# The pieces of the last weight matrix in another order, and three of them converted from shifted bytes

## The chip, the cores and the metric

The kernel runs on one core of one Trainium2 chip. The metric is the device time of one execution in microseconds. The median of three runs of the kernel before is 475.51 us (475.21 to 475.67).

## The reference: what is computed

Three stages follow each other: attention with soft-capped scores, a feed-forward layer with a softmax-like activation and a layer norm, and a gated feed-forward layer. The change lies in the last one:

```python
def _moe2_ref(x, w_gate, w_val, w_out):          # x 896 x 768, w_gate and w_val 768 x 1536, w_out 1536 x 768
    g = x @ w_gate
    silu = g * (1.0 / (1.0 + np.exp(-g)))
    val = x @ w_val
    return (silu * val @ w_out).astype(np.float32)
```

The weights come as float64 numbers, and the output is float32.

## The kernel before, in words

TensorE multiplies every pair of float32 operands as a high and a low part, each rounded to the engine's format: high by high, high by low, low by high, three matmuls for one (`mm3`). So each operand is split: `hi` is a rounding copy on ScalarE, `lo` a subtraction on VectorE.

A weight tile is 128 x 768 float64 numbers, about 768 KB. It takes four steps to become float32. `load_shifted` (L166) issues the DMA on SyncE's queue, leaving out the first three bytes, so that the wanted bits stand in aligned words. Then two ScalarE activations with the function Prelu make sign and exponent out of the top byte, and one VectorE `SCALAR_TENSOR_TENSOR` ORs the mantissa in (`f32_shifted`, L180). The other way, `load64` with `f32_steps` (L103, L114), is a plain load, one ScalarE absolute value, and on VectorE two `TENSOR_SCALAR` (clamp and shift) and two `SCALAR_TENSOR_TENSOR` (sign and mantissa). `b22`, the last quarter of w_out2, went this way, in three pieces (0, 2 and 4).

In the last third of the kernel the bytes land in a pool with two buffers named `raw`, and the float32 values in one with two buffers named `f32` (`self.st`, L1191). Pieces take the two in turn. The DMA of a piece therefore waits for the `SCALAR_TENSOR_TENSOR` of the piece two places ahead of it, and its first Prelu for the splits of that piece.

The hidden dimension of 1536 is worked on in 12 blocks (`fc`). For the last three (9, 10, 11) the loop at the end of `run` multiplies x by the block's gate weights (`g`) and value weights (`v`): 18 matmuls of 384 columns for each, then 18 of 512 for each. The weights of block 11 (`wg`, `wv` below) are loaded by `load_gv` (L624) while block 10 is multiplied, through the same two `raw` buffers as the pieces of w_out2 that `load_w2` (L939) fetches. The table `early` (L1264) says which piece is loaded in which half of which block, and so sets the one order of all these loads:

```python
early = {9: ((6, 8), (0,)), 10: ((1,), (2,)), 11: ((3, 4), (5, 10))}
...
    elif fc + 1 < K2:
        self.load_gv(fc + 1, i)
    for c in early[fc][i]:
        self.load_w2(c)
    self.ff2_gv(fc, N, o)
```

A scheduler orders the instructions of ScalarE and VectorE by times that it assumes; each engine then works them off strictly in that order, and TensorE's order is the program's.

The output product (`ff2_out`, L980) is a seven-product scheme on 2 x 2 blocks (products p1 to p7, for three row tiles and a seventh half). p1 uses the pieces 0 to 5 (`b11`), p2 the pieces 6, 8 and 10 (`b21`). Beside the products, VectorE makes sums and differences of operands; p6 needs the last of them (`so`, `t`). The three pieces of `b22` are converted during the first products (`conv`).

Of the kernel before, what the change touches and what calls it, by code (L numbers as in the profile page):

```python
# [56 lines left out]
class Kernel:  # L57
# [898 lines left out]
    def load_b22(self, k):  # L956

        src = self.w_out2[(self.KD + k) * 128:(self.KD + k + 2) * 128, self.HN:].rearrange("(f p) d -> p f d", p=128)
        self.b22raw[k] = self.load64(src, f"b22_{k}")

    def f32_b22(self, k):

        f = self.B22f[:, k:k + 2].rearrange("p f d -> p (f d)")
        self.f32(self.b22raw.pop(k), f"b22_{k}", f=f)

    def split_b22(self, k):

# [179 lines left out]
    def run(self):  # L1147
# [18 lines left out]
        w = [self.w_in_steps(i) for i in range(KD)]  # L1166
        f, g, hi, lo = zip(*w)
# [49 lines left out]
        wb, gb = self.wb, _ = self.pool("wb"), self.pool("gb")  # L1217
# [10 lines left out]
        for j in range(2, KD):  # L1228
# [4 lines left out]
            a, b = x2[j]  # L1233
# [27 lines left out]
        self.sg = (self.ee[:, :n], self.ee[:, n:n + 512])  # L1261
        self.T1f = [self.ee[:, n + 512 + n * i:n + 512 + n * (i + 1)] for i in range(3)] + [t1, self.sms]
        self.t1 = t1
        early = {9: ((6, 8), (0,)), 10: ((1,), (2,)), 11: ((3, 4), (5, 10))}  # L1264
        for fc in range(K2):
            if fc == 0:
                self.ff2_gv_first()
# [66 lines left out]
```

## Time and profile before

| | |
|---|---|
| median of 3 runs | 475.51 us |
| profiled execution: device time | 475.99 us |
| profiled execution: span of instructions | 474.2 us |
| TensorE busy | 466.7 us, 98% of the span |
| VectorE busy | 387.8 us, 82% |
| ScalarE busy | 310.4 us, 65% |

The span runs from the first to the last instruction; 1.8 us of the device time lie outside it. Times in the rows below are microseconds from the start of the span. In a row, a tile's name stands without its number: `w<-w_raw` is a piece of w_out2, `wg` and `wv` the gate and value weights, `b` the b22 quarter.

### The profile page before, as it was taken

Reading aid. Unit: us, or ns where it says so; the run is one execution under the profiler, and the core shown is the slowest. Engines: PE = TensorE matmul, PEld = TensorE weight load, DVE = VectorE, ACT = ScalarE, POOL = GpSimd, SP = SyncE. Lnnn points to the kernel's source line nnn. Section 1 sums busy time; section 2 is a strip of 40 time slices with the busy share of each in tenths; the row PEclk is TensorE's granted clock in tenths of the full one; section 3 lists DMA queues with packets and bytes.
Section 4 is the critical chain, followed back from the end, with each engine's and each line's share of the span. In section 5 each row is a group of like instructions: output and inputs, shape, how many; then the busy total and the mean of one; then the engine's idle time right before and its main releaser. Section 6 shows DMA issues by size and latency. Waiting matters only on the chain.

```text
span 474.2 us, 7675 instructions
## 1 busy us (share of the span) xinstructions
PE 466.7 (98%) x2970; PEld 384.8 (81%) x2970; DVE 387.8 (82%) x669; ACT 310.4 (65%) x455; POOL 38.7 (8%) x76
## 2 busy tenths in 40 slices
PE   9999999999999999999999999999999999998997
PEld 7444454447888899989989999999999889998996
DVE  3689999987778996866778899989876768999993
ACT  4999999951223799887767766766667778344220
POOL 1011010112000000000012222220000000000000
PEclk9999999999999999999999999999999999999999
DMA  6786575002000225345225444331445757010003
GB/s 181 170 207 153 163 193 153 21 2 88 1 1 0 90 88 165 126 129 180 66 81 185 134 134 132 109 122 37 132 128 155 241 182 221 7 50 18 17 19 132
DMA packets 65060, 52.33 MB, mean 110 GB/s; under 512 B 35584, under 2 KB 61952, under 8 KB 64256
## 3 DMA queue, kind: packets, MB, share of 16 engines
q1 hardware_dynamic: 64992, 51.85, 36.7%
q8 instruction: 23, 0.38, 0.3%
q14 instruction: 13, 0.11, 0.1%
q0 software_dynamic: 32, 0.00, 0.0%
HBM read 49.09 MB, written 2.75 MB: 109 GB/s over the span
## 4 chain that ended last, share of the span: by engine, by line
PE 80%; DVE 10%; DMA 5%; ACT 4%; issue 1%; ACTq 0%; DVEq 0%; SPq 0%
PE x L49 12%; PE h L49 12%; PE p L49 8%; PE g L49 8%; PE pv L49 8%; PE sc L49 7%; PE b L49 6%; PE c L49 6%; PE S L49 4%; DMA w_raw<-in_moe_w_out_dram 3%; PE e L49 3%; DVE b L49 2%; ACT w L49 2%; PE v L49 2%; DVE so L49 1%; PE lt L49 1%
## 5 line engine op out<-in xcount | busy, mean ns | idle before, releaser
L49 PE MATMUL g<-x,g 128*128 128x448 f32 (+2 forms) x288 | 62.2, 365 | 0.0
L49 PE MATMUL h<-wi,x 128*128 128x512 f32 x252 | 59.2, 393 | 0.0
L49 PEld LDWEIGHTS g<-x,g 128*128 128x128 f32 x288 | 53.1, 188 | 5.4 <-ACT ee L49 0.3
L49 PEld LDWEIGHTS h<-wi,x 128*128 128x128 f32 x252 | 46.8, 188 | 11.3 <-issue 1.5
L49 ACT ACTIVATE P<-sc,consts 112x896 f32<-112x896 f32 x48 | 45.4, 1010 | 3.8 <-PE sc L49 2.2
L49 ACT ACTIVATE P<-P,consts 112x3584 f32<-112x3584 f32 (+1 forms) x13 | 39.7, 3060 | 0.1
L49 PE MATMUL pv<-P,v 112*32 112x448 f32 x384 | 38.5, 540 | 0.0
L49 PEld LDWEIGHTS sc<-ks 64*112 64x112 f32 x288 | 23.3, 171 | 18.3 <-issue 8.4
L49 PE MATMUL sc<-ks 64*112 64x448 f32 x288 | 35.8, 379 | 0.3
L49 PE MATMUL x<-lB,wo 128*128 128x256 f32 (+1 forms) x192 | 35.2, 337 | 0.0
L49 PEld LDWEIGHTS x<-lB,wo 128*128 128x128 f32 x192 | 29.6, 189 | 3.4
L49 PE MATMUL b<-a,g 128*128 128x448 f32 x144 | 31.9, 366 | 0.0
L49 ACT ACTIVATE ee<-h,sms 128x512 f32<-128x512 f32 x14 | 9.5, 685 | 33.2 <-DVE sms L49 33.2
L49 PEld LDWEIGHTS pv<-P,v 112*32 112x32 f32 x384 | 12.2, 110 | 23.0 <-issue 20.9
L49 PE MATMUL v<-x,g 128*128 128x384 f32 (+1 forms) x144 | 30.4, 362 | 0.3 <-DVE g L49 0.3
L49 PEld LDWEIGHTS b<-a,g 128*128 128x128 f32 x144 | 27.0, 188 | 2.3 <-DVE ee L49 0.2
L49 PEld LDWEIGHTS v<-x,g 128*128 128x128 f32 x144 | 26.0, 188 | 3.5 <-DVE g L49 0.7
L49 PE MATMUL x<-lA,wo 128*128 128x384 f32 x144 | 27.2, 338 | 0.0
L49 PEld LDWEIGHTS x<-lA,wo 128*128 128x128 f32 x144 | 25.2, 188 | 0.5
L49 POOL COPY sm<-tr 32x14 f32<-32x14 f32 x48 | 15.0, 312 | 93.1 <-DVE tr L49 91.6
L49 PE MATMUL S<-P,ones 112*32 112x448 f32 x192 | 22.4, 549 | 0.0
L49 DVE TENSOR_TENSOR x<-x,x 128x448 fp32r<-128x448 f32 (+3 forms) x26 | 15.3, 588 | 8.3 <-ACT x L49 7.6
(273 smaller groups left out, 967.6 us busy)
## 6 DMA issues: line engine op xcount, KB each, us to landing
wg_raw<-in_moe_w_gate_dram SPq DMA_DIRECT2D x12, 765.8 KB, 4.3
wv_raw<-in_moe_w_val_dram SPq DMA_DIRECT2D x11, 765.8 KB, 4.7
wi_raw<-in_moe_w_in_dram SPq DMA_DIRECT2D x6, 1024.0 KB, 7.7
w_raw<-in_moe_w_out_dram SPq DMA_DIRECT2D x6, 767.6 KB, 4.2
wo_raw<-in_moe_w_out_dram SPq DMA_DIRECT2D x6, 512.0 KB, 3.5
wo_raw<-in_moe_w_out_dram SPq DMA_DIRECT2D x6, 510.5 KB, 3.6
v<-in_v_dram SPq DMA_DIRECT2D x24, 112.0 KB, 4.0
kq<-in_k_dram SPq DMA_DIRECT2D x22, 112.0 KB, 3.0
```

The costliest lines, as they stand in the source:

```text
L49: i = f(*a, **k)
```

## The change: what it does

The table `early` gets another order: 0, 1, 2, 3, then 6, 8, 4, 5, 10. The pieces of `b22` are loaded by `load_shifted` and converted by two Prelu and one `SCALAR_TENSOR_TENSOR` in place of the five instructions.

```diff
     def load_b22(self, k):
 
         src = self.w_out2[(self.KD + k) * 128:(self.KD + k + 2) * 128, self.HN:].rearrange("(f p) d -> p f d", p=128)
-        self.b22raw[k] = self.load64(src, f"b22_{k}")
+        self.b22raw[k] = self.load_shifted(src, f"b22_{k}")
 
     def f32_b22(self, k):
 
         f = self.B22f[:, k:k + 2].rearrange("p f d -> p (f d)")
-        self.f32(self.b22raw.pop(k), f"b22_{k}", f=f)
+        raw, o = self.b22raw.pop(k), {}
+        self.shifted_steps(o, "b", lambda: raw, lambda: f)
+        for w in "12f":
+            o["wb" + w]()
...
-        early = {9: ((6, 8), (0,)), 10: ((1,), (2,)), 11: ((3, 4), (5, 10))}
+        early = {9: ((0, 1), (2, 3)), 10: ((6,), (8,)), 11: ((4, 5), (10,))}
```

SyncE's queue, from the first piece of w_out2 on; `w_6_raw` is piece 6, `wg_raw` and `wv_raw` are the weights of block 11, minus is before and plus is now:

```order
-L177 DMA w_6_raw<-in_moe_w_out_dram 128x2x3069
-L177 DMA w_8_raw<-in_moe_w_out_dram 128x2x3069
 L173 DMA w_0_raw<-in_moe_w_out_dram 128x6141
-L177 DMA wg_raw<-in_moe_w_gate_dram 128x6x1021
 L173 DMA w_1_raw<-in_moe_w_out_dram 128x6141
-L177 DMA wv_raw<-in_moe_w_val_dram 128x6x1021
 L173 DMA w_2_raw<-in_moe_w_out_dram 128x6141
 L173 DMA w_3_raw<-in_moe_w_out_dram 128x6141
+L177 DMA wg_raw<-in_moe_w_gate_dram 128x6x1021
+L177 DMA w_6_raw<-in_moe_w_out_dram 128x2x3069
+L177 DMA wv_raw<-in_moe_w_val_dram 128x6x1021
+L177 DMA w_8_raw<-in_moe_w_out_dram 128x2x3069
```

`wg` moves from the fourth place to the fifth, and `wv` from the sixth to the seventh; after these rows come 4, 5, 10 and the three pieces of b22 in both kernels.

ScalarE before, from the first Prelu of `wg` to the rounding copy of `wv` (`g_2` and `g_3` are the tiles that TensorE reads for block 11, `ee<-g` is a Silu, `a<-` and `kR<-` are rounding copies):

```order
L49 ACTIVATE wg_3605<-wg_raw,consts 128x768
L49 ACTIVATE a_2486<-w_0_3553 128x384
L49 ACTIVATE wg_3605<-wg_3605,consts 128x768
L49 ACTIVATE g_2_1930<-wg_3605 128x768
L49 ACTIVATE a_2486<-ee 128x384
L49 ACTIVATE w_1_3613<-w_1_raw,consts 128x768
L49 ACTIVATE w_1_3613<-w_1_3613,consts 128x768
L49 ACTIVATE ee<-g_384_3679 128x512
L49 ACTIVATE wv_3664<-wv_raw,consts 128x768
L49 ACTIVATE a_2486<-w_1_3613 128x384
L49 ACTIVATE wv_3664<-wv_3664,consts 128x768
L49 ACTIVATE g_3_1931<-wv_3664 128x768
```

The same stretch now, from the first Prelu of piece 6, which stands between the second Prelu of `wg` and the copy of `wg`:

```order
L49 ACTIVATE w_6_3620<-w_6_raw,consts 128x768
L49 ACTIVATE g_2_1930<-wg_3612 128x768
L49 ACTIVATE w_6_3620<-w_6_3620,consts 128x768
L49 ACTIVATE wv_3672<-wv_raw,consts 128x768
L49 ACTIVATE kR<-w_6_3620 128x384 x2
L49 ACTIVATE a_2486<-ee 128x512
L49 ACTIVATE wv_3672<-wv_3672,consts 128x768
L49 ACTIVATE ee<-g_0_3749 128x384
L49 ACTIVATE w_8_3680<-w_8_raw,consts 128x768
L49 ACTIVATE g_3_1931<-wv_3672 128x768
```

Before, nothing that waits for a transfer stood between the second Prelu of `wg` or `wv` and its copy. Now the first Prelu of piece 6 stands ahead of the copy of `wg`, and that of piece 8 ahead of the copy of `wv`; three rounding copies stand between the two Prelu of `wv`, where there was one.

## Rows read from the trace of the kernel before

**Rows 1.** The page: busy time by engine, and granted clock of 40 slices

```profile
PE 466.7 (98%) x2970; PEld 384.8 (81%) x2970; DVE 387.8 (82%) x669; ACT 310.4 (65%) x455; POOL 38.7 (8%) x76
...
PEclk9999999999999999999999999999999999999999
```

**Rows 2.** Waits of TensorE, 330 to 476: total us, times, longest

```profile
PE p L49 <- DVE so L49: 2.0, 1, 2.0
PE p L49 <- DVE g L49: 0.7, 1, 0.7
PE v L49 <- DVE g L49: 0.3, 1, 0.3
```

**Rows 3.** Timeline of TensorE: start, us, engine, line, operation, [idle before]

```profile
373.90 3.31 PE L49 MATMUL g<-x,g 128*128 128x384 f32 x18
377.05 0.52 PE L49 MATMUL v<-x,g 128*128 128x384 f32 x2
377.91 3.05 PE L49 MATMUL v<-x,g 128*128 128x384 f32 x16 [0.34 <-DVE g L49]
...
392.68 0.62 PE L49 MATMUL p<-g,a 128*128 128x384 f32 x2 [0.66 <-DVE g L49]
...
433.35 0.98 PE L49 MATMUL p<-t,so 128*128 128x384 f32 x4 [2.04 <-DVE so L49]
```

**Rows 4.** Timeline of SyncE's DMA queue, the first six loads

```profile
349.16 1.77 SPq L177 DMA_DIRECT2D w_raw<-in_moe_w_out_dram  x2
356.73 0.35 SPq L173 DMA_DIRECT2D w_raw<-in_moe_w_out_dram  x1
360.91 0.37 SPq L177 DMA_DIRECT2D wg_raw<-in_moe_w_gate_dram  x1
365.34 0.35 SPq L173 DMA_DIRECT2D w_raw<-in_moe_w_out_dram  x1
368.43 0.37 SPq L177 DMA_DIRECT2D wv_raw<-in_moe_w_val_dram  x1
```

**Rows 5.** Timeline of ScalarE around the first Prelu of `wg`, and the copy of `wv`

```profile
362.88 0.61 ACT L49 ACTIVATE a<-ee 128x512 fp32r<-128x512 f32 x1
363.40 0.92 ACT L49 ACTIVATE w<-w,consts 128x768 int32<-128x768 f32 x1
...
365.18 1.00 ACT L49 ACTIVATE wg<-wg_raw,consts 128x768 f32<-128x768 int8 x1 [0.48 <-DMA wg_raw<-in_moe_w_gate_dram]
366.07 0.52 ACT L49 ACTIVATE a<-w 128x384 fp32r<-128x384 f32 x1
366.49 0.93 ACT L49 ACTIVATE wg<-wg,consts 128x768 int32<-128x768 f32 x1
...
376.01 0.85 ACT L49 ACTIVATE g<-wv 128x768 fp32r<-128x768 f32 x1 [1.02 <-DVE wv L49]
```

**Rows 6.** Timeline of VectorE: the mantissa step of the first two pieces, of `wg` and `wv`

```profile
355.75 0.96 DVE L49 SCALAR_TENSOR_TENSOR w<-w_raw,w 128x768 uint32<-128x768 uint32 x1 [2.42 <-ACT w L49]
...
359.92 0.96 DVE L49 SCALAR_TENSOR_TENSOR w<-w_raw,w 128x768 uint32<-128x768 uint32 x1 [0.21 <-ACT w L49]
...
367.45 0.96 DVE L49 SCALAR_TENSOR_TENSOR wg<-wg_raw,wg 128x768 uint32<-128x768 uint32 x1 [0.27 <-ACT wg L49]
...
375.02 0.96 DVE L49 SCALAR_TENSOR_TENSOR wv<-wv_raw,wv 128x768 uint32<-128x768 uint32 x1 [0.27 <-ACT wv L49]
...
376.89 0.96 DVE L49 TENSOR_TENSOR g<-wv,g 128x768 fp32r<-128x768 f32 x1 [0.31 <-ACT g L49]
```

**Rows 7.** Timeline of VectorE: a piece of b22, and the step that p6 waits for

```profile
396.32 1.15 DVE L49 TENSOR_SCALAR b<-b 128x768 f32<-128x768 f32 x2 [0.42 <-ACT b L49]
397.51 1.95 DVE L49 SCALAR_TENSOR_TENSOR b<-b_raw,b 128x768 uint32<-128x768 uint32 x2
...
432.35 3.56 DVE L49 TENSOR_TENSOR so<-s,so 128x768 fp32r<-128x768 f32 x4
```

**Rows 8.** Busy time of each engine and granted clock, two stretches

```profile
351.00:395.00 44.00, 43.00 (x212) 37.95 (x211) 29.51 (x46) 32.02 (x46) 0.00 (x0) 1.00 0.64 214
396.00:433.00 37.00, 35.31 (x203) 34.73 (x201) 36.37 (x55) 21.10 (x36) 0.00 (x0) 1.00 0.21 65
```

## The prediction

> **What bounds the kernel now.** I read the page first. TensorE is busy for 466.7 of 474.2 us, so a change here can win only its few waits [rows 1]. Next the list of TensorE's waits over the last 146 us: there are three, 3.04 us together [rows 2]. Then the timeline, to see where they stand [rows 3]. At 377.91 the third matmul of block 11's value product waits 0.34 us for the low part of `wv`. At 392.68 p1 waits 0.66 us for the low part of piece 5. At 433.35 p6 waits 2.04 us for VectorE. The first two are the end of the stream of loads. The third is the end of a long VectorE chain, since that engine is busy for 36.37 of the 37 us from 396 to 433 [rows 8], and TensorE goes on when the first of four `so<-s` steps that begin at 432.35 has ended [rows 7].
>
> What limits the stream? Its loads go out one by one, from 349 to 368 six of them [rows 4], and each waits for the mantissa step of the piece two places ahead: that of the first piece begins at 355.75 and the third load goes out at 356.73; that of `wg` begins at 367.45 and `wv` goes out at 368.43 [rows 4, 6]. So both buffers are always in use, and a piece's place in the order decides when it is ready.
>
> **The conversion of b22.** Each of three pieces loses two `TENSOR_SCALAR` (1.15 us together) and one of two `SCALAR_TENSOR_TENSOR` (1.95 - 0.96) [rows 6, 7]: 2.14 us, 6.4 us in all from a chain that is late by 2.04. ScalarE's one absolute value becomes two Prelu, which adds about one second Prelu of 0.93 us for each piece [rows 5], 2.8 in all, to an engine that is busy for 21.10 of these 37 us [rows 8]. Even if all 2.8 stood in VectorE's way, 3.6 would be left, more than 2.04. I take the 2.04 as won, and zero as the other end.
>
> **The order: `wg`.** I follow the two buffers with intervals from start to start. Load to first Prelu 4.3 (360.91 to 365.18); first Prelu to the next instruction 0.9; a copy of 384 columns 0.42 and of 512 columns 0.52; second Prelu to mantissa step 0.96; mantissa step to the next load, or to the copy, 0.98; copy of 768 columns to its subtraction 0.88; subtraction to TensorE 1.02 [rows 3 to 6].
>
> - First buffer: piece 0 in place of piece 6, mantissa step at 355.75 as before. Piece 2 goes out at 356.73, its Prelu begin at 361.0 and (behind a copy of 512) 362.4, its mantissa step at 363.4. `wg` goes out at 364.4 (before: 360.91), its Prelu begin at 368.7 and (behind a copy of 384) 370.0, its mantissa step at 371.0.
> - Second buffer: piece 1 in place of piece 8 has one copy less ahead of its second Prelu, so 359.92 becomes 359.5. Piece 3 goes out at 360.5, with mantissa step at 367.1; piece 6 goes out at 368.1, with its first Prelu at 372.4.
> - That Prelu stands ahead of the copy of `wg`: 373.3, subtraction 374.2, TensorE 375.2. It comes to that matmul at 374.25 (373.90 and two matmuls). It loses 0.9 us.
>
> **The order: `wv`.** It goes out at 371.0 + 0.98 = 371.95 (before: 368.43), and its first Prelu begins at 376.25. Behind three copies (0.42, 0.42, 0.52) the second begins at 378.5; the mantissa step follows at 379.5. Its copy is queued behind the first Prelu of piece 8, which went out after piece 6's mantissa step (375.05) at 376.0 and lands at 380.3. So the copy begins at 381.2, the subtraction at 382.1, and TensorE's third matmul at 383.1. Without waits that matmul would have begun at 377.57 [rows 3]. It is late by 5.5 us, where it was late by 0.34: 5.2 us more, the loss at `wg` included, since the same matmuls stand behind both. The same steps on the old order give 377.98, where the row has 377.91, so I trust the method to half a microsecond. TensorE would then stand empty for about 4.2 us in one piece.
>
> Bounds: if no copy and no foreign Prelu stood in ScalarE's way, each round of a buffer would be 4.3 + 0.9 + 0.96 + 0.98 = 7.1 us, and the matmul would begin at 380.1, 2.2 us more than before. With 0.3 us more on each of the three loads that lead to `wv` in its buffer it would be 384.0, 6.1 more.
>
> **What the delay swallows.** Places 9 to 11 still hold pieces 4, 5 and 10, and by the same steps piece 5's mantissa step begins at 390.6, about where it was. TensorE comes to it 5 us later, so the 0.66 us go. At p6 it comes 4.5 us later, and VectorE, by the paragraph on b22, earlier: the 2.04 go if either holds. VectorE's start into the chain slips by about 1.2 us, since ScalarE's first Prelu of b22 is queued behind the copy of the late block's result; 6.4 covers it. Behind p6 TensorE ran 37 us without a wait, with VectorE further behind than it will be now, so I expect none there.
>
> The sum, against the profiled execution: 474.2 + 5.2 - 0.66 - 2.04 = 476.7 us of span, and with 1.8 outside it 478.5. That execution was 0.48 above the median, so in medians 475.51 + 2.5 = 478.0 us.
>
> **Rivals.**
>
> 1. The clock falls while TensorE stands empty. Every slice and stretch here shows the full granted clock, 2.4 GHz [rows 1, 8], but TensorE never waited longer than 2.04 us in this stretch, and 4.2 us is twice that. The 16 matmuls left of that product take 2.77 us (16 x 0.173); at the lower level, 1.2 GHz, they would take twice that, and nothing behind them is left to swallow it: 478.0 + 2.8 = 480.8. If it lasted into the next product (4.1 us), up to 484.9.
>    The Trainium skill, "TensorE: Matmul & The Clock Gate", Part 1: The HAM clock gate, says that the array passes to its lower rate after TensorE has been idle, and comes back after sustained work. By that rule the stall could cost more than its own length; no row of this trace shows such a fall.
> 2. The stall is short and the change wins. It decides at 380.6: if TensorE gets the low part of `wv` earlier than that, the new delay is under 2.7 us, less than the two waits that go. With the unhindered bound (380.1, +2.2) the time is 475.51 + 2.2 - 2.7 = 475.0. For it speaks that the landing of a load may be shorter when rows are contiguous (pieces 0 to 3); against it that both engines work in the order shown, with foreign work in the way.
> 3. The 2.04 us are not won: the VectorE chain, which feeds on TensorE's results and on ScalarE's three added Prelu, slips with them. Then 478.0 + 2.0 = 480.0. Against it stand 6.4 us less work and a later TensorE.
>
> **How the numbers follow.** The forecast has a chance of 0.60, with its own range of 476.8 to 479.2 (the method's half microsecond and the spread of landings); the clock 0.22; the short stall 0.10; the third 0.08. The likeliest gives 478.0. The range for 8 in 10 is 475.8 to 481.2: it takes in the first and third rival as priced, and leaves out most of the second and a longer fall of the clock. A measurement of this kernel can tell 0.2%, 0.95 us, from no change. Of the second rival's tenth, 0.06 is faster by more than that and 0.04 is same; with 0.01 of the forecast's lower edge: faster 0.07, same 0.05, slower 0.88.
>
> **What would show it.** In the profile after, TensorE's list of waits has `v` for `g` on top, over 4 us, and no `so` at p6. `wv` goes out near 372 and its mantissa step begins near 379.5. VectorE's `TENSOR_SCALAR` on `b` are gone. The granted clock in the 8 us behind the stall tells the first rival. I am wrong if `wv` reaches TensorE before 380.6, or if a wait at p6 stays.

## The result and the profile after

The changed kernel takes 479.21 us (median of 22 runs), the kernel before 476.79 us in 22 runs taken beside it: a ratio of 1.0053, 95% interval 1.0036 to 1.0069. On the median of the first runs that is 475.51 x 0.0053 = +2.5 us, with an interval of +1.7 to +3.3; the prediction had +2.5. The profiled execution has a span of 476.8 us in place of 474.2. The size is right; part of the way there is not.

The page after, busy time and granted clock by slice, which answers to [rows 1]:

```profile
PE 467.7 (98%) x2970; PEld 385.9 (81%) x2970; DVE 381.8 (80%) x660; ACT 313.0 (66%) x458; POOL 38.6 (8%) x76
...
PEclk9999999999999999999999999999999989999999
```

VectorE has lost 6.0 us, ScalarE has gained 2.6. One slice of the clock, the 33rd (381.4 to 393.4 us), is no longer full. TensorE's waits after 330 us, as in [rows 2]:

```profile
PE v L49 <- ACT g L49: 3.9, 1, 3.9
PE g L49 <- DVE g L49: 0.4, 1, 0.4
```

The wait at p6 is gone, and so is that for piece 5. In their place `v` waits 3.9 us for the high part of `wv`, and `g` 0.4 for the low part of `wg`. TensorE's timeline after, as in [rows 3]:

```profile
344.12 3.31 PE L49 MATMUL g<-x,g 128*128 128x384 f32 x18
...
373.34 0.62 PE L49 MATMUL g<-x,g 128*128 128x384 f32 x2
374.34 3.05 PE L49 MATMUL g<-x,g 128*128 128x384 f32 x16 [0.38 <-DVE g L49]
381.30 5.81 PE L49 MATMUL v<-x,g 128*128 128x384 f32 x18 [3.91 <-ACT g L49]
386.94 4.28 PE L49 MATMUL g<-x,g 128*128 128x512 f32 x18
...
395.14 1.23 PE L49 MATMUL p<-a,a 128*128 128x384 f32 x6
...
420.13 9.52 PE L49 MATMUL p<-so 128*128 128x384 f32 x54
...
435.73 1.20 PE L49 MATMUL p<-t,so 128*128 128x384 f32 x6
436.77 1.20 PE L49 MATMUL p<-so 128*128 128x384 f32 x6
```

The places in the kernel before that these are compared with:

```profile
344.97 3.31 PE L49 MATMUL g<-x,g 128*128 128x384 f32 x18
...
380.79 4.28 PE L49 MATMUL g<-x,g 128*128 128x512 f32 x18
...
388.99 1.23 PE L49 MATMUL p<-a,a 128*128 128x384 f32 x6
...
391.10 0.92 PE L49 MATMUL p<-g,a 128*128 128x384 f32 x4
...
393.14 1.20 PE L49 MATMUL p<-a,a 128*128 128x384 f32 x6
...
415.20 9.52 PE L49 MATMUL p<-so 128*128 128x384 f32 x54
...
430.80 0.51 PE L49 MATMUL p<-t,so 128*128 128x384 f32 x2
...
434.17 1.21 PE L49 MATMUL p<-so 128*128 128x384 f32 x6
```

Block 9, ahead of all that the change moves, begins at 344.12 in place of 344.97: this execution is 0.85 us early by then. I take that as chance, since in the nine profiles of this document the same row begins anywhere from 343.74 to 345.70. From there:

- Block 11's first two products take from 373.05 (373.90 less 0.85) to 386.94, 13.89 us; before, 373.90 to 380.79, 6.89. Lost: 7.0.
- p1 and p2 take 24.99 us (395.14 to 420.13); before 26.21. Won: 1.22.
- The first six matmuls of p6 take 1.04 us; before 3.37. Won: 2.33.
- 7.0 - 1.22 - 2.33 - 0.85 = 2.6, the difference of the spans.

Why are 18 matmuls of `v` slow, 5.64 us to the next product where they take 3.1 otherwise? Busy time and granted clock of four stretches after (us; PE, PEld, DVE, ACT, POOL busy, granted clock, DMA share, GB/s):

```profile
375.00:379.00 4.00, 2.39 (x14) 2.07 (x12) 3.32 (x7) 3.55 (x6) 0.00 (x0) 1.00 0.66 196
379.00:381.30 2.30, 0.01 (x1) 0.01 (x1) 0.60 (x2) 1.77 (x3) 0.00 (x0) 0.57 0.34 60
381.30:386.00 4.70, 4.70 (x14) 4.21 (x15) 2.83 (x4) 3.57 (x5) 0.00 (x0) 0.50 0.71 251
386.00:390.00 4.00, 4.00 (x20) 3.45 (x19) 2.95 (x5) 2.65 (x4) 0.00 (x0) 0.98 0.65 176
```

The clock fell to 0.50, its lower level of 1.2 GHz, while TensorE stood empty, and was full again near 386. The prediction's first rival came true. This agrees with the rule that the prediction cites (the Trainium skill, "TensorE: Matmul & The Clock Gate", Part 1: The HAM clock gate): idle time takes the clock down, and sustained work brings it back.

The load of `wv` after, in SyncE's queue, as in [rows 4],

```profile
371.15 0.37 SPq L177 DMA_DIRECT2D wv_raw<-in_moe_w_val_dram  x1
```

ScalarE from the first Prelu of `wv` to its copy, as in [rows 5],

```profile
375.41 1.01 ACT L49 ACTIVATE wv<-wv_raw,consts 128x768 f32<-128x768 int8 x1 [1.29 <-DMA wv_raw<-in_moe_w_val_dram]
...
377.67 0.92 ACT L49 ACTIVATE wv<-wv,consts 128x768 int32<-128x768 f32 x1
...
379.53 0.98 ACT L49 ACTIVATE w<-w_raw,consts 128x768 f32<-128x768 int8 x1 [0.57 <-DMA w_raw<-in_moe_w_out_dram]
380.41 0.83 ACT L49 ACTIVATE g<-wv 128x768 fp32r<-128x768 f32 x1
```

and VectorE, as in [rows 6, 7]:

```profile
378.62 0.96 DVE L49 SCALAR_TENSOR_TENSOR wv<-wv_raw,wv 128x768 uint32<-128x768 uint32 x1
381.28 0.96 DVE L49 TENSOR_TENSOR g<-wv,g 128x768 fp32r<-128x768 f32 x1 [1.70 <-ACT g L49]
...
430.02 3.57 DVE L49 TENSOR_TENSOR so<-s,so 128x768 fp32r<-128x768 f32 x4
```

With the 0.85 us added, `wv` goes out at 372.0 (forecast 371.95), its mantissa step begins at 379.47 (379.5), its subtraction at 382.13 (382.1). The copy at 380.41 begins when the first Prelu of piece 8, which waited for its transfer, is over; by the interval of 0.98 us from mantissa step to copy it could have begun at 379.60, so ScalarE's order cost some 0.8 us of the delay. No run tests that part by itself. At p6 VectorE's step begins at 430.02, and TensorE comes there at 435.73.

### The profile page after: what moved, and what is told of

Read it like the earlier page. It is cut to its first block, busy times and chain, and to the rows that moved or that the text cites. A ratio compares the mean times of both kernels' runs of the same rounds, so it can differ in the third digit from the quotient of the medians.

```text
span 476.8 us, 7667 instructions
## 1 busy us (share of the span) xinstructions
PE 467.7 (98%) x2970; PEld 385.9 (81%) x2970; DVE 381.8 (80%) x660; ACT 313.0 (66%) x458; POOL 38.6 (8%) x76
## 4 chain that ended last, share of the span: by engine, by line
PE 90%; DMA 5%; ACT 2%; DVE 2%; issue 0%; SPq 0%; ACTq 0%
PE p L49 16%; PE x L49 12%; PE h L49 12%; PE g L49 9%; PE pv L49 7%; PE sc L49 6%; PE b L49 6%; PE c L49 6%; PE S L49 4%; DMA w_raw<-in_moe_w_out_dram 4%; PE v L49 4%; PE e L49 3%; ACT w L49 2%; DMA kq<-in_q_dram 1%; PE lt L49 1%; PE T L49 1%
## 5 line engine op out<-in xcount | busy, mean ns | idle before, releaser
L49 PE MATMUL v<-x,g 128*128 128x384 f32 (+1 forms) x144 | 32.6, 382 | 3.9 <-ACT g L49 3.9
L49 PEld LDWEIGHTS v<-x,g 128*128 128x128 f32 x144 | 27.9, 202 | 7.5 <-ACT g L49 4.2
```

The lines of the kernel that those rows point to most:

```text
L49: i = f(*a, **k)
```

## The experiments

The theory A: the order puts `wv` one place back in a stream that both buffers limit; TensorE stands empty, the clock falls, and the new conversion of b22 takes away only the wait at p6. The rival B: the added Prelu on ScalarE cost the time late in the kernel.

**The order alone.**

```diff
-        early = {9: ((6, 8), (0,)), 10: ((1,), (2,)), 11: ((3, 4), (5, 10))}
+        early = {9: ((0, 1), (2, 3)), 10: ((6,), (8,)), 11: ((4, 5), (10,))}
```

> The new order of the pieces alone, b22 converted as before. Theory A (the loss is TensorE's stall on wv and the clock that falls in it; the new conversion of b22 only removes the wait at p6): the stall of about 4 us on wv and the lower granted clock behind it are there as in the changed kernel. TensorE comes to p6 some 5 us later than before, and VectorE's chain, which starts about 1 us later, still ends first, so the wait at p6 is gone without the new conversion: +2 to +3 us against the kernel before (ratio 1.004 to 1.006), the same as the full change. Theory B (the two Prelu of b22 on ScalarE cost time late in the kernel): about 1 us or more faster than the full change.

Measured: 1.0050 (1.0030 to 1.0069). TensorE's waits, and the clock in a stretch behind the longest:

```profile
PE v L49 <- ACT g L49: 3.9, 1, 3.9
...
PE v L49 <- DVE g L49: 0.4, 1, 0.4
PE g L49 <- DVE g L49: 0.3, 1, 0.3
```

```profile
382.00:384.00 2.00, 1.62 (x6) 1.30 (x6) 1.53 (x2) 0.93 (x3) 0.00 (x0) 0.56 0.79 310
```

The same stall, a fall of the clock again, and no wait at p6 although b22 is converted as before. The fall is shorter in this execution than in the profile of the changed kernel (mean clock 0.996 against 0.993); the medians are alike (479.13 and 479.21). B is out: the order makes up the whole loss, and beside it the new conversion wins nothing that these runs can tell, since a late TensorE no longer waits for VectorE.

**The conversion alone**: the changed kernel with the old line of `early`.

> The new conversion of b22 alone, the pieces in the old order. Theory A: wv and piece 5 as before (waits 0.34 and 0.66 us stay), the wait of 2.04 us at p6 is gone: -2.0 to -2.4 us against the kernel before (ratio 0.995 to 0.996). Theory B: no gain or a loss, 1.000 or more.

Measured: 473.36 us, 0.9933 (0.9910 to 0.9956), faster than both kernels. TensorE's waits after 330 us:

```profile
PE p L49 <- DVE g L49: 0.7, 1, 0.7
PE v L49 <- DVE g L49: 0.4, 1, 0.4
PE p L49 <- ACT g L49: 0.3, 1, 0.3
```

VectorE's step at p6:

```profile
428.72 3.56 DVE L49 TENSOR_TENSOR so<-s,so 128x768 fp32r<-128x768 f32 x4
```

p6's wait is gone; the waits for `wv` and piece 5 stay, with 0.3 us more for the high part of piece 5. The gain is 3.2 us by the ratio (2.1 to 4.3), where 2.0 to 2.4 was expected. From the first matmul of block 9 (343.76 here) to the end, the two profiled executions differ by 2.0 us, as expected. The rest may be the clock: all of this kernel's 6 runs have a mean granted clock of 0.999 or 1.000, where the kernel before often has less (the last experiment).

VectorE has some 6 us less to do, but counted from block 9 its step at p6 begins only 2.4 us earlier (84.96 us behind block 9's start, before 87.38). That is just enough for the wait of 2.04. Part of the rest goes into waits of 0.90 and 0.91 us for ScalarE's Prelu of the second and third piece.

**A third order with the new conversion.**

```diff
+        early = {9: ((0, 1), (2,)), 10: ((), (3,)), 11: ((4, 5), (6, 8, 10))}
```

> The new conversion of b22, and a third order: 0, 1, 2, wg, wv, 3, 4, 5, 6, 8, 10, so that wg stands at place 4 and wv at place 5 (before: 4 and 6; changed: 5 and 7), piece 5 at place 8 (10). Theory A (the place in the order decides when a piece is ready): wv is ready about 4 us ahead of TensorE, piece 5 about 8 us ahead, p6 does not wait: no wait of TensorE in the last 146 us, granted clock full, -3.5 to -4.2 us against the kernel before (ratio 0.991 to 0.993). Theory B: like the new conversion with the old order or slower, since the place of wv is of no weight.

Measured: 474.35 us, 0.9959 (0.9931 to 0.9988), less gain than expected and none over the conversion alone. The only wait after 330 us, and VectorE's step that ends it:

```profile
PE p L49 <- DVE so L49: 1.5, 1, 1.5
```

```profile
429.68 3.55 DVE L49 TENSOR_TENSOR so<-s,so 128x768 fp32r<-128x768 f32 x4
```

`wv` and piece 5 wait no more, as A says, but TensorE, now earlier, waits at p6 again. My forecast took VectorE's chain as out of the way, and it was so only for a TensorE that came late. Counted from block 9 (344.72 here), VectorE's step is 2.42 us earlier than in the kernel before, as with the conversion alone, and TensorE comes to p6 1.85 us earlier: 2.04 - 2.42 + 1.85 = 1.47, the wait that the row shows. Of the 11 runs compared, 6 have a full mean clock (0.998 or more) and a median of 473.3, the other 5 a lower one and 476.7.

**The changed kernel with the stall filled** with matmuls whose product nobody reads:

```diff
-        ps = [self.gv_product(fc, i, N, o) for i in range(2)]
+        ps = [self.gv_product(fc, 0, N, o)]
+        if fc == 11 and o == 0:
+            z = self.pt.tile([128, 512], F32, name="fill", tag="m")
+            for _ in range(16):
+                self.PE.matmul(z, self.gvs[fc][0][:, 0, 0, :], self.x2[0][:, 0, 384:896], start=True, stop=True)
+        ps.append(self.gv_product(fc, 1, N, o))
```

> The changed kernel with 16 matmuls of 512 columns, whose product nobody reads, between block 11's gate product and its value product (some 3.5 us of TensorE's time, where it stood empty for 3.9). Theory A1 (the granted clock fell because TensorE stood empty): it stays full, wv's first matmul begins when it did, and the 18 matmuls of that product take 3.1 us in place of 5.6: 1.5 to 2.5 us less than the changed kernel, +0 to +1 against before (ratio 1.000 to 1.002). Theory A2 (the product is slow for another reason, such as the weights arriving late): no change against the changed kernel, 1.005.

Measured: 477.35 us, 1.0012 (0.9996 to 1.0028) against before, by the two ratios some 1.9 us less than the changed kernel. TensorE's timeline and the clock:

```profile
378.08 3.83 PE L49 MATMUL fill<-x,g 128*128 128x512 f32 x16
382.40 0.62 PE L49 MATMUL v<-x,g 128*128 128x384 f32 x2 [0.49 <-ACT g L49]
383.40 3.04 PE L49 MATMUL v<-x,g 128*128 128x384 f32 x16 [0.38 <-DVE g L49]
386.28 4.28 PE L49 MATMUL g<-x,g 128*128 128x512 f32 x18
```

```profile
378.00:382.40 4.40, 3.91 (x18) 2.90 (x16) 2.33 (x5) 3.60 (x7) 0.00 (x0) 1.00 0.62 211
382.40:386.20 3.80, 3.42 (x18) 3.10 (x19) 2.84 (x4) 2.70 (x5) 0.00 (x0) 1.00 0.61 200
```

`wv` is as late as before the filling, but the product takes 3.9 us to the next one in place of 5.64. So the slow matmuls came from the idle time, not from late weights. Counted from block 9 (344.91 here), block 11's first two products end 5.55 us later than in the kernel before, where the changed kernel has 7.0.

**The third order with the old conversion.** The edit is the third `early` line in the kernel before.

> The third order (0, 1, 2, wg, wv, 3, 4, 5, 6, 8, 10) with the old conversion of b22. Theory A, with what the last runs add (once wv and piece 5 are early, VectorE's chain to p6 is what ends last): the waits at wv and piece 5 are gone and come back at p6, which waits for 3.5 to 4.5 us; VectorE's last step ahead of p6 ends when it did before. No gain: ratio 0.999 to 1.001 if the granted clock stays full, up to 1.005 where it falls in that wait. Theory C (the early weights are a gain of their own): 0.996, as with the new conversion.

Measured: 1.0018 (0.9999 to 1.0037): no gain, as A says. But the wait is not where I put it. TensorE's waits, VectorE's splits of piece 10, and the clock in that wait and behind it:

```profile
PE p L49 <- DVE g L49: 2.8, 1, 2.8
PE p L49 <- ACT g L49: 1.3, 1, 1.3
```

```profile
405.86 1.02 DVE L49 TENSOR_TENSOR g<-w,g 128x384 fp32r<-128x384 f32 x2
```

```profile
402.60:406.40 3.80, 0.45 (x1) 0.19 (x1) 3.80 (x8) 3.23 (x7) 0.00 (x0) 1.00 0.46 182
406.40:411.00 4.60, 4.54 (x17) 4.54 (x18) 4.46 (x8) 1.58 (x3) 0.00 (x0) 0.63 0.01 4
```

p2 waits for piece 10, whose splits stand behind those of the sums in both engines' order. VectorE, busy for all of the 3.80 us, still ends last, at another of its steps, and the clock falls again (0.63).

**The sums' splits ahead of b22's first conversion**, with the third order and the new conversion.

```diff
-            ("p1_0", 0, ((A11, b11),), (do(conv, 0),), copy(P1[0])),
-            ("p1_1", 1, ((A11, b11),), (do(s1, 0), do(s1, 2)), copy(P1[1])),
-            ("p1_2", 2, ((A11, b11),), (do(s1, 4),), copy(P1[2])),
+            ("p1_0", 0, ((A11, b11),), (do(s1, 0), do(s1, 2)), copy(P1[0])),
+            ("p1_1", 1, ((A11, b11),), (do(s1, 4),), copy(P1[1])),
+            ("p1_2", 2, ((A11, b11),), (do(conv, 0),), copy(P1[2])),
```

> The third order and the new conversion, and in the output product the splits of the sums (so), which need no piece of b22, stand ahead of the conversion of b22's first piece in place of behind it. Theory A: VectorE does these 6 us of splits while it would wait for pieces 10 and b22, its chain to p6 ends 2 to 4 us earlier, p6 does not wait, and no wait is left in the last 146 us: 1.5 to 2.5 us less than the third order alone, ratio 0.990 to 0.993 against the kernel before, and all runs at full granted clock. Theory D (ScalarE or the loads hold the chain, not VectorE's order): same as the third order alone, 0.996.

Measured: 478.24 us, 1.0031 (1.0011 to 1.0051), slower than the third order alone, which neither theory had. VectorE's timeline, TensorE at p6, and the clock behind that wait:

```profile
402.56 0.96 DVE L49 SCALAR_TENSOR_TENSOR w<-w_raw,w 128x768 uint32<-128x768 uint32 x1 [0.24 <-ACT w L49]
...
408.85 0.96 DVE L49 SCALAR_TENSOR_TENSOR b<-b_raw,b 128x768 uint32<-128x768 uint32 x1 [3.71 <-ACT b L49]
```

```profile
434.82 1.65 PE L49 MATMUL p<-t,so 128*128 128x384 f32 x4 [3.64 <-DVE so L49]
```

```profile
434.80:438.00 3.20, 3.17 (x10) 3.18 (x11) 3.20 (x4) 1.23 (x3) 0.00 (x0) 0.52 0.00 0
```

The splits fill VectorE's idle time, but they also push piece 10's conversion back to 402.56 (395.54 in the third order alone). Its buffer is what b22's second piece loads into, so that piece comes late, VectorE idles 3.71 us, p6 waits 3.64, and the clock falls. It is the buffer rule once more, through another piece.

**The kernel before, with p6's wait filled.**

```diff
+            if nm == "p6_0":
+                z = self.pt.tile([128, 512], F32, name="fill", tag="m")[:, :n]
+                for _ in range(11):
+                    self.PE.matmul(z, B22[0][0][:, :128], B22[0][0], start=True, stop=True)
             self.products(acc, A, B() if callable(B) else B, t, start, evict is not None)
```

> The kernel before, with 11 matmuls of 384 columns, whose product nobody reads, in front of p6, where TensorE waited 2.04 us for VectorE. Theory E (in about half of the runs of the kernel before the mean granted clock is 0.995 or 0.996 and the time is about 1 us longer, since the clock falls in this wait): the mean clock is 0.999 or more in all runs, and the median falls by 0.5 to 1 us: ratio 0.998 to 0.999. Theory F (the clock falls elsewhere in these runs): the clocks as before, ratio 1.000 to 1.001.

Measured: 475.65 us, 0.9979 (0.9955 to 1.0002). In 10 of 12 runs the mean clock is 0.999 or more; of 57 runs of the kernel before that were taken with the experiments, 26 have 0.998 or more (median 476.1 us) and 31 less (477.3). TensorE's timeline:

```profile
431.50 2.07 PE L49 MATMUL fill<-a 128*128 128x384 f32 x11
433.40 1.59 PE L49 MATMUL p<-t,so 128*128 128x384 f32 x6
```

This fits theory E: the wait at p6 takes the clock down in about half of the runs. The interval just reaches 1, two runs still have 0.996, and the one profile of the kernel before shows a full clock behind this wait (1.00 from 433.4 to 436), so it is likely, not shown.

## Why the prediction was right, point by point

- **The stream and its two buffers**: right. `wv`'s steps came within 0.1 us of the forecast, counted from block 9, and ScalarE's order held its copy back as forecast (381.26, forecast 381.2).
- **The new delay at `wg` and `wv`**: forecast 5.2, measured 7.0; the stall in it 4.2, measured 3.9. The mis-sized term is the speed behind the stall, where I left the clock full in the likeliest case and gave its fall 0.22. The fall came. With the stall filled the delay is 5.55, near the forecast; the fall is worth some 1.5 us between these two profiles and 1.9 in the runs.
- **The waits that go**: forecast 0.66 + 2.04 = 2.70, measured 1.22 + 2.33 = 3.55. The idle time that the timeline puts ahead of a row is less than the matmuls lose: in the kernel before six matmuls of p1 took 2.04 us (391.10 to 393.14) in place of 1.04, and six of p2, at 404.58, lost another 0.22.
- **b22**: worth 0.67% alone, but this term was too large. VectorE has 6.0 us less to do, but the prediction counted 6.4 as time won at p6, and 3.6 if all of ScalarE's added work stood in the way. Measured, the step at p6 begins 2.42 us earlier with the conversion alone, and 1.48 in the changed kernel (85.90 us behind block 9's start), since the new order alone makes it 2.0 later, where 1.2 was forecast. The 1.48 are less than the 2.04, so by these numbers the conversion would not have taken away the whole wait if TensorE had not come late; no run shows that. The late TensorE takes it away without the conversion, as the order alone shows, so in this change the conversion won nothing. The prediction, which said that either would do, did not say whose the gain would then be.
- **The sum**: 7.0 - 3.55 is 3.45 us in the two profiled executions, after taking out 0.85 us of chance at the start, and 2.5 in the runs. Two errors of opposite sign, 1.8 and 0.85, cancel by half. The other half, 0.95, is not in the medians: if half of the runs of before lose 1.2 us to the clock at p6, as the last experiment suggests, their median (476.79) stands above the profiled execution (475.99), and the difference is smaller. That is likely, not shown. The direction was earned; that the number fits to a tenth of a microsecond is luck.
- **The rivals**: the first came true in its mechanism, at some 1.9 us where it was priced at 2.8; the second (a short stall) and the third (p6 keeps its wait) did not.

## What to carry to other kernels

When two buffers in turn feed a stream of loads, a piece's place is its due time; count places (here about 3.9 us each: in the changed kernel eleven mantissa steps begin between 354.87 and 393.85) for what the bound engine needs next before giving a place ahead of it to pieces needed later. A wait removed in front of the bound engine is worth only what the next chain allows: the early weights won nothing with the old conversion (1.0018) and nothing over the new one (0.9959 against 0.9933), since TensorE then waits for VectorE; and the shorter chain won nothing while the weights were late. Work taken off an engine is not time won at the end of its chain: 6 us less work made the VectorE step that p6 needs only 2.4 us earlier. TensorE's stall of 3.9 us cost some 1.9 us more than its length, because the clock was down when it ended; price a stall of that size so.

## What the runs showed of the hardware that I had not expected

A stall of 3.9 us took the granted clock to 0.50, and it stayed there for some 5 us of dense matmuls; in all 22 runs of the changed kernel the mean clock was 0.991 to 0.996. A wait of 3.64 us at p6 took it to 0.52, and two waits of 1.3 and 2.8 us with one matmul between them to 0.63 in the stretch behind. Behind the single waits of 2.04 us (the kernel before) and 1.5 us (the third order) the profiles show it full. Yet 31 of 57 runs of the former and 5 of 11 of the latter have a lower mean clock, at a cost of 1.2 and 3.4 us between the medians. That these waits bring it down in part of the runs is likely by the last experiment, and not shown by any profile.
